# Attention then a skipping mixture of experts: one slot group closed early, 1/rms as a power on GpSimd, k^T v in small jobs

## The chip, the cores and the metric

The kernel runs on one core of a Trainium2 chip. The metric is the device time of one execution in microseconds, about 1.8 us more than the span in the profile.

The kernel before took 557.6 to 561.4 us on the chip of the first four experiments, 580.1 to 583.7 on the chip of the next four, and 579.6 to 582.2 on that of the last four. I call the first kind quiet and the others stuttering; what they differ in is shown below. The timed result of the change is, to judge by before's 558.88, from a quiet chip, while the profile of the kernel before, from which the prediction was made, is an execution of 581.39 us. So times are compared only within one call, or through their ratios to the kernel before.

## The reference

```python
kv = einsum('bhsd,bhse->bhde', k, v)            # 8 batches, 8 heads, 576 rows, 64 wide
out = einsum('bhsd,bhde->bhse', q, kv)
x = out / sqrt(mean(out*out, -1) + 1e-6) * g_norm   # then (B, H, S, D) -> (4608, 512)
do = x @ w_skip > 0                             # rows that compute
e = argmax(x @ w_gate), gate = softmax at e     # 8 experts
out[do] = x + gate * (relu(x @ w1[e]) @ w2[e])  # 512 -> 1024 -> 512, f32
```

## The kernel before

Attention goes through 36 units. A unit turns q on TensorE, multiplies it with the batch's k^T v (the gate logits ride along as nine more columns per head), squares on ScalarE, sums on VectorE and scales. Units are software pipelined: in step n the program issues the matmuls of unit n and the scaling of unit n-1. There are two PSUM buffers o_ps, so the matmuls of unit n+2 wait for the scaling of unit n.

```python
def scale(n):                                   # (cut to the core)
    nc.vector.tensor_reduce(out=rs, in_=sq, axis=AX.X, op=ALU.add)
    nc.scalar.activation(out=rs, in_=rs, func=ACT.Sqrt, scale=1.0 / D, bias=eps_t)

def norm(n):
    nc.vector.reciprocal(out=rs, in_=rs)
    nc.vector.tensor_tensor(out=xn, in0=heads(ps, 0, D), in1=r4, op=ALU.mult)
    nc.vector.tensor_tensor(out=lps[g][...], in0=heads(ps, D, KD), in1=r4, op=ALU.mult)
    nc.gpsimd.tensor_tensor(out=xb[...], in0=xn, in1=g_b, op=ALU.mult)
...
ends = [8, 18, 26, 32, 36]                      # groups of row tiles for gating
...
# at the first step of batch b: all 144 matmuls of k^T v of batch b + 1, then a VectorE copy
at(n, "pe", lambda b=b: state(b + 1))
```

After each group of row tiles, `choose`, `rank`, `number` and `settle` find the expert and the slot of every row (VectorE and small matmuls). After the last group the rows of each expert's 384 slots are gathered from memory, 108 small matmuls place the gate values, and eight experts run, each two layers of f32 matmuls.

Of the kernel before, what the change touches and what calls it, by code (L numbers as in the profile page):

```python
# [16 lines left out]
def kernel(  # L17
# [54 lines left out]
    wpool_a = ctx.enter_context(tc.tile_pool(name="wpool_a", bufs=1))  # L72
    attn = ctx.enter_context(ExitStack())
    setup = attn.enter_context(tc.tile_pool(name="setup", bufs=1))
    kv_pool = attn.enter_context(tc.tile_pool(name="kv", bufs=3))
    q_pool = attn.enter_context(tc.tile_pool(name="q", bufs=3))
    kvn_pool = attn.enter_context(tc.tile_pool(name="kvn", bufs=6))
# [3 lines left out]
    gat_pool = attn.enter_context(tc.tile_pool(name="gat", bufs=2))  # L81
    ps_o = attn.enter_context(tc.tile_pool(name="ps_o", bufs=2, space=bass.MemoryType.PSUM))
    ps_kv = attn.enter_context(tc.tile_pool(name="ps_kv", bufs=1, space=bass.MemoryType.PSUM))
    ps_q = attn.enter_context(tc.tile_pool(name="ps_q", bufs=1, space=bass.MemoryType.PSUM))
    ps_g = attn.enter_context(tc.tile_pool(name="ps_g", bufs=1, space=bass.MemoryType.PSUM))
# [52 lines left out]
    ut = setup.tile([P, P], BF16)  # L138
    nc.vector.tensor_scalar(out=ut[:, :], in0=row128_i[:, :], scalar1=part_f[:, 0:1],
                            scalar2=None, op0=ALU.is_ge)  # L140
    row128 = setup.tile([P, P], FP32)
    nc.vector.tensor_copy(out=row128[:, :], in_=row128_i[:, :])
    ones = setup.tile([P, P], BF16)
    nc.vector.memset(ones[:, :], 1.0)
    eps_t = setup.tile([P, 1], FP32)
    nc.vector.memset(eps_t[:, :], 1e-6)
    eorder = setup.tile([P, E], FP32)
# [21 lines left out]

    gw_b = setup.tile([D, 2, 4, G], FP32)  # L170
# [19 lines left out]

    w_sb = {}
# [11 lines left out]
    def state(b):  # L203

        kt, vt = kts.pop(b), vts.pop(b)
        ps = ps_kv.tile([P, 2, 512], FP32, tag="kv", name="kv_ps")
        for u in range(2):
            for c in range(C):
                for w in range(2):
                    for a in range(2):  # L210
                        r = slice(a * 64, (a + 1) * 64)
                        nc.tensor.matmul(  # L212
                            out=ps[w * 64:(w + 1) * 64, a, u * D:(u + 1) * D],
                            lhsT=kt[r, 2 * u + w, c, :], rhs=vt[r, 2 * u + w, c, :],
                            start=(c == 0), stop=(c == C - 1), skip_group_check=True)
        kvn = kvn_pool.tile([P, 2, 2, KD], FP32, tag="kvn", name="kvn")
        nc.vector.tensor_copy(out=kvn[:, :, :, 0:D],
                              in_=ps[:, :, 0:2 * D].rearrange("p a (u d) -> p a u d", u=2))
        kv_ps[b], kvns[b] = ps, kvn
# [44 lines left out]
    ends = [8, 18, 26, 32, 36]  # L264
# [37 lines left out]
    def values(n):  # L302
# [14 lines left out]
        sq = att_pool.tile([P, 2, 4, D], FP32, tag="sq", name="sq", bufs=2)  # L317
        nc.scalar.activation(out=sq[:, :, :, :], in_=heads(ps, 0, D), func=ACT.Square)  # L318
        ops[n] = (ps, sq)

    def scale(n):
        ps, sq = ops[n]
        rs = att_pool.tile([P, 2, 4], FP32, tag="rs", name="rs")
        nc.vector.tensor_reduce(out=rs[:, :, :], in_=sq[:, :, :, :], axis=AX.X, op=ALU.add)  # L324
        nc.scalar.activation(out=rs[:, :, :], in_=rs[:, :, :], func=ACT.Sqrt, scale=1.0 / D,  # L325
                             bias=eps_t[:, 0:1])
        rss[n] = rs

    def norm(n):
# [3 lines left out]
        nc.vector.reciprocal(out=rs[:, :, :], in_=rs[:, :, :])  # L333
        r4 = rs[:, :, :].unsqueeze(3)
        xn = att_pool.tile([P, 2, 4, D], FP32, tag="xn", name="xn")
        nc.vector.tensor_tensor(out=xn[:, :, :, :], in0=heads(ps, 0, D),  # L336
                                in1=r4.to_broadcast([P, 2, 4, D]), op=ALU.mult)
        g = sum(2 * nq >= x for x in ends)
        t0 = 2 * nq - ([0] + ends)[g]
        if t0 == 0 and u == 0:  # L340
            lps[g] = gat_pool.tile([P, TG, H, G], FP32, tag="lp", name="lp")
        nc.vector.tensor_tensor(out=lps[g][:, t0:t0 + 2, 4 * u:4 * u + 4, :],  # L342
                                in0=heads(ps, D, KD), in1=r4.to_broadcast([P, 2, 4, G]),
                                op=ALU.mult)
        if i is None:
            if u == 0:
                xbs[b, i] = xb_pool.tile([P, 2, DM], FP32, tag="xl", name="xl", bufs=1)
            xb = xbs[b, i]
        else:
            if i == 0 and u == 0:  # L350
                xbs[b, 0] = xb_pool.tile([P, NQ, 2, DM], FP32, tag="xb", name="xb")
            xb = xbs[b, 0][:, i, :, :]
        nc.gpsimd.tensor_tensor(  # L353
            out=xb[:, :, 4 * u * D:(4 * u + 4) * D].rearrange("p r (h d) -> p r h d", d=D),
            in0=xn[:, :, :, :],
            in1=g_b[:, :].unsqueeze(1).unsqueeze(1).to_broadcast([P, 2, 4, D]), op=ALU.mult)
        if u == 0:
            return None
# [85 lines left out]
    def columns(t0, nt, colid, val, pieces, pool):  # L444

        ohc = pool.tile([P, NT, NCOL], BF16, tag="ohc", name="ohc")[:, 0:nt, :]
# [3 lines left out]
        bv = pool.tile([P, NT, pieces, NCOL], BF16, tag=f"bv{pieces}", name="bv")[:, 0:nt, :, :]  # L450
# [6 lines left out]
    def place(ps, bv, t0, nt, pieces):  # L457

        for t in range(nt):
            for i in range(pieces):  # L460
                nc.tensor.matmul(out=ps, lhsT=oha_k[:, t0 + t, :], rhs=bv[:, t, i, :],
                                 start=(t == 0 and i == 0), stop=(t == nt - 1 and i == pieces - 1))

    def settle(g):
        t0, t1 = ([0] + ends)[g], ends[g]
        sp = ps_g.tile([P, 512], FP32, tag="g", name="slot_ps")[:, 0:NCOL]
        place(sp, bvs.pop(g), t0, t1 - t0, 2)
        sps[g] = sp

    def add_slots(g):  # L470
        nc.vector.tensor_tensor(out=srow[:, :], in0=srow[:, :], in1=sps.pop(g), op=ALU.add)

    load_kv(0)
# [4 lines left out]

    with tc.manual_schedule():
        state(0)  # L480
        state_t(0)
        turn(0)
        state_m(0)
        state_s(0)
        todo = {}

        def at(step, part, job):
            todo.setdefault((step, part), []).append(job)

        def jobs(step, part):  # L490
            for job in todo.pop((step, part), []):
                job()

        starts = {}
        for n, (_, b, i, _) in enumerate(units):
            if i is not None:
                starts.setdefault(b, n)
        for b, n in starts.items():
            if b + 1 < B:
                at(n, "pe", lambda b=b: state(b + 1))  # L500
                at(n + 1, "pe", lambda b=b: state_t(b + 1))
                at(n + 2, "pe", lambda b=b: state_m(b + 1))
                at(n + 3, "pe", lambda b=b: state_s(b + 1))
            at(n + 1, "pe", lambda b=b: turn_8(b))

            def loads(b=b):
                load_kv(b + 3)
                load_q(b + 2)
                if b + 2 == B - 1:
                    load_weights(0, wpool_a)  # L510
            at(n, "end", loads)

        n = 0
        while n <= NU or todo:
            if n + 1 < NU:
                turn(n + 1)
            if n < NU:
                values(n)
            jobs(n, "pe")
            if 1 <= n <= NU:  # L520
                store = norm(n - 1)
                if store:
                    at(n + 2, "end", store)
            if n < NU:
                scale(n)
            jobs(n, "dve")
            if n % 2 == 0 and n in ends:
                g = ends.index(n)
                choose(g)
                at(n + 1, "pe", lambda g=g: rank(g))  # L530
                at(n + 1, "dve", lambda g=g: number(g))
                at(n + 2, "pe", lambda g=g: settle(g))
                at(n + 2, "dve", lambda g=g: add_slots(g))
            jobs(n, "end")
            n += 1
# [3 lines left out]
    with tc.tile_pool(name="wpool_b", bufs=2) as wpool_b, \  # L539
         tc.tile_pool(name="gather", bufs=1) as gather_pool, \  # L540
         tc.tile_pool(name="ffn", bufs=2) as ffn, \
         tc.tile_pool(name="slot", bufs=1) as slot_pool, \
         tc.tile_pool(name="ps_i", bufs=2, space=bass.MemoryType.PSUM) as ps_i, \
         tc.tile_pool(name="ps_h", bufs=3, space=bass.MemoryType.PSUM) as ps_h, \
         tc.tile_pool(name="ps_y", bufs=3, space=bass.MemoryType.PSUM) as ps_y:

        def slot_rows():

            rows = slot_pool.tile([P, NCOL], I32, tag="rows", name="rows")
            nc.vector.tensor_single_scalar(out=rows[:, :], in_=srow[:, :], scalar=float(N),  # L550
                                           op=ALU.add)
            src = slot_pool.tile([P, NCOL], I32, tag="src", name="src")
            nc.vector.tensor_single_scalar(out=src[:, :], in_=rows[:, :], scalar=N - 1, op=ALU.min)
            return rows, src
# [15 lines left out]
        def slot_gates(colid):  # L570
            gp = ps_i.tile([P, 512], FP32, tag="xp", name="gate_ps")[:, 0:NCOL]
# [49 lines left out]
        def experts(group, colid):  # L621
# [3 lines left out]
            if group == "first":  # L625
                gates()
# [61 lines left out]
```

## Time and profile before

| | before |
|---|---|
| time, median | 558.88 us (558.57 to 559.84) |
| span of the profiled execution | 579.5 us |
| last scaling ends | 179.0 us |
| gap to layer 1 | 49 us in the profile (46.7 to its first matmul, at 225.7) |
| experts | 8 x 42.7 us |

The prediction shows the stages, waits and chain. What is still needed is the cost of one operation of each kind in a unit. The columns of the page's groups: line, engine, operation, output and input, their sizes, count | busy us, mean ns of one | idle time of the engine before them and what ended it.

```profile
L353 POOL TENSOR_TENSOR xb<-xn,g_b 128x512 f32<-128x512 f32 x32 | 40.6, 1269 | 116.0 <-DVE xn L336 115.9
L336 DVE TENSOR_TENSOR xn<-o_ps,rs 128x512 f32<-128x512 f32 x36 | 24.9, 692 | 4.2 <-DVE rs L333 0.5
L324 DVE TENSOR_REDUCE rs<-sq 128x8 f32<-128x512 f32 x36 | 24.4, 679 | 4.7 <-ACT sq L318 4.5
L325 ACT ACTIVATE rs<-rs,eps_t 128x8 f32<-128x8 f32 x36 | 10.8, 301 | 74.5 <-DVE rs L324 74.3
```

GpSimd is idle for 116 us before its one product per unit, and the square root is small but stands in ScalarE's order. Both invite the change: take work from ScalarE and VectorE and give it to GpSimd.

### The profile page before, as it was taken

The page shows a single profiled execution, that of the slowest core. Times are in us where ns is not written, and L with a number is a line of the kernel's source. Part 1 is how long each engine was busy: PE and PEld are TensorE (multiplying, and loading weights), DVE is VectorE, ACT ScalarE, POOL GpSimd, SP SyncE. Part 2 cuts the span into 40 slices and gives each one's busy share as a digit, 9 for nine tenths or more (in the row PEclk, how much of TensorE's full clock was granted, in tenths as well). Part 3 has the DMA queues.
Part 4 walks back from the last instruction along what each step waited for, and adds up shares of the span by engine and source line. Part 5 has one row for each costly group of instructions (what it writes and reads, how often), then busy time and mean ns, then how long its engine had stood idle before and what let it go on. Part 6 is the DMA issues. An engine that isn't in the chain of part 4 may idle for free.

```text
span 579.5 us, 8786 instructions
## 1 busy us (share of the span) xinstructions
PE 466.6 (81%) x3820; PEld 280.7 (48%) x3820; DVE 135.1 (23%) x351; ACT 95.2 (16%) x204; POOL 102.0 (18%) x108
## 2 busy tenths in 40 slices
PE   2576776679641316999999999999999999999990
PEld 2465655557531204545545545545545545545540
DVE  0143664742878301002002002011011011010010
ACT  0243443233342000200200100100200101101100
POOL 0022333231334770001001001001010010010010
PEclk9589877675785556999999999999999999999996
DMA  8997877583246993043044044044044000000000
GB/s 277 396 390 259 314 255 253 155 301 67 61 88 175 395 416 138 1 163 132 32 163 153 13 163 170 3 163 164 3 161 166 2 20 10 1 36 12 2 36 15
DMA packets 33131, 82.91 MB, mean 143 GB/s; under 512 B 3409, under 2 KB 3409, under 8 KB 33088
## 3 DMA queue, kind: packets, MB, share of 16 engines
q1 hardware_dynamic: 25216, 61.87, 29.7%
q0 software_dynamic: 5152, 15.66, 7.9%
q10 hardware_dynamic: 2720, 4.77, 3.5%
q8 instruction: 32, 0.52, 0.4%
q14 instruction: 11, 0.09, 0.0%
HBM read 68.21 MB, written 15.73 MB: 145 GB/s over the span
## 4 chain that ended last, share of the span: by engine, by line
PE 73%; DVE 10%; issue 6%; DMA 5%; ACT 2%; POOL 1%; POOLq 0%; DVEq 0%; ACTq 0%
PE hps L602 29%; PE yps L609 28%; PE o_ps L313 4%; PE kv_ps L212 3%; PE q_ps L278 2%; PE xp L591 2%; DMA q<-in_q_dram 2%; DVE xn L336 2%; PE kv_ps L247 2%; DMA xg<-out_dram,src 2%; DMA wraw<-in_moe_w_gate_dram 1%; DVE rs L324 1%; PE kv_ps L237 1%; DVE oha_k L439 1%; DVE lg L381 1%
## 5 line engine op out<-in xcount | busy, mean ns | idle before, releaser
L602 PE MATMUL hps<-xt,w 128*128 128x384 f32 x512 | 168.7, 488 | 0.0
L609 PE MATMUL yps<-w,ht 128*128 128x512 f32 x384 | 166.1, 592 | 0.0
L602 PEld LDWEIGHTS hps<-xt,w 128*128 128x128 f32 x512 | 96.8, 191 | 64.5 <-issue 0.8
L609 PEld LDWEIGHTS yps<-w,ht 128*128 128x128 f32 x384 | 73.0, 190 | 90.1 <-issue 88.0
L611 DVE SCALAR_TENSOR_TENSOR xg<-yps,gate,xg 128x512 f32<-128x512 f32 x24 | 18.0, 751 | 308.2 <-PE yps L609 308.2
L604 ACT ACTIVATE ht<-hps 128x384 f32<-128x384 f32 x64 | 31.4, 490 | 328.8 <-PE hps L602 284.6
L614 POOL DMA_INDIRECT out_dram<-xg,rows x24 | 23.7, 986 | 325.8 <-DVE xg L611 319.9
L353 POOL TENSOR_TENSOR xb<-xn,g_b 128x512 f32<-128x512 f32 x32 | 40.6, 1269 | 116.0 <-DVE xn L336 115.9
L313 PE MATMUL o_ps<-kvn,qT 64*64 64x73 f32 x512 | 30.7, 271 | 12.5 <-DVE lp L342 10.8
L212 PE MATMUL kv_ps<-v,k 64*64 64x64 f32 x1152 | 23.2, 245 | 18.3 <-DMA v<-in_v_dram 9.9
L313 PEld LDWEIGHTS o_ps<-kvn,qT 64*64 64x64 f32 x512 | 24.9, 168 | 20.9 <-DVE lp L342 13.3
L278 PE MATMUL q_ps<-ident,q 128*128 128x128 f32 x128 | 27.3, 350 | 9.4 <-DMA q<-in_q_dram 4.8
L212 PEld LDWEIGHTS kv_ps<-v,k 64*64 64x64 f32 x1152 | 22.3, 161 | 18.7 <-issue 18.7
L313 PE MATMUL o_ps<-kvs,qT 64*64 64x73 f32 x512 | 30.2, 271 | 0.0
L581 POOL DMA_INDIRECT xg<-out_dram,src x24 | 24.5, 1022 | 13.0 <-issue 7.0
L591 PE MATMUL xp<-ident,xg 128*128 128x128 f32 x96 | 16.5, 314 | 12.0 <-DMA xg<-out_dram,src 12.0
L278 PEld LDWEIGHTS q_ps<-ident,q 128*128 128x128 f32 x128 | 18.8, 177 | 15.1 <-ACT q L297 5.6
L336 DVE TENSOR_TENSOR xn<-o_ps,rs 128x512 f32<-128x512 f32 x36 | 24.9, 692 | 4.2 <-DVE rs L333 0.5
L324 DVE TENSOR_REDUCE rs<-sq 128x8 f32<-128x512 f32 x36 | 24.4, 679 | 4.7 <-ACT sq L318 4.5
L313 PEld LDWEIGHTS o_ps<-kvs,qT 64*64 64x64 f32 x512 | 24.4, 168 | 0.0
L325 ACT ACTIVATE rs<-rs,eps_t 128x8 f32<-128x8 f32 x36 | 10.8, 301 | 74.5 <-DVE rs L324 74.3
L318 ACT ACTIVATE sq<-o_ps 128x512 f32<-128x512 f32 x36 | 21.6, 599 | 8.3 <-PE o_ps L313 7.6
(102 smaller groups left out, 234.0 us busy)
## 6 DMA issues: line engine op xcount, KB each, us to landing
w<-in_moe_w_dram SPq DMA_DIRECT2D x16, 2048.0 KB, 8.4
k<-in_k_dram SPq DMA_DIRECT2D x8, 1152.0 KB, 11.4
v<-in_v_dram SPq DMA_DIRECT2D x8, 1152.0 KB, 12.0
q<-in_q_dram SPq DMA_DIRECT2D x8, 1152.0 KB, 9.1
out_dram<-xb POOLq DMA_DIRECT2D x8, 512.0 KB
out_dram<-xb ACTq DMA_DIRECT2D x8, 512.0 KB, 4.4
out_dram<-xl POOLq DMA_DIRECT2D x2, 256.0 KB
out_dram<-xl ACTq DMA_DIRECT2D x2, 256.0 KB, 4.0
```

What stands on the lines that cost most here:

```text
L212: nc.tensor.matmul(out=ps[w * 64:(w + 1) * 64, a, u * D:(u + 1) * D], lhsT=kt[r, 2 * u + w, c, :], rhs=vt[r, 2 * u + w, c, :], start=(c == ...
L278: nc.tensor.transpose(out=ps[:, w, hf, :], in_=qts[b][:, 2 * u + w, c:c + 2, :], identity=ident[:, :])
L313: nc.tensor.matmul(out=ps[hf * 64:(hf + 1) * 64, r, (2 * w + a) * KD:(2 * w + a + 1) * KD], lhsT=qT[rows, w, hf, a * 64:(a + 1) * 64], rhs ...
L324: nc.vector.tensor_reduce(out=rs[:, :, :], in_=sq[:, :, :, :], axis=AX.X, op=ALU.add)
L336: nc.vector.tensor_tensor(out=xn[:, :, :, :], in0=heads(ps, 0, D), in1=r4.to_broadcast([P, 2, 4, D]), op=ALU.mult)
L353: nc.gpsimd.tensor_tensor(out=xb[:, :, 4 * u * D:(4 * u + 4) * D].rearrange("p r (h d) -> p r h d", d=D), in0=xn[:, :, :, :], in1=g_b[:, : ...
L581: nc.gpsimd.indirect_dma_start(out=xg[:, c, :], out_offset=None, in_=out[:, :], in_offset=bass.IndirectOffsetOnAxis(ap=src[:, col:col + 1] ...
L591: nc.tensor.transpose(out=xp[:, dc, :], in_=xg[:, c, dc * P:(dc + 1) * P], identity=ident[:, :])
L602: nc.tensor.matmul(out=hps[:, :], lhsT=w1[:, dc, f * P:(f + 1) * P], rhs=xt[:, dc, :], start=(dc == 0), stop=(dc == DC - 1))
L604: nc.scalar.activation(out=ht[:, f, :], in_=hps[:, :], func=ACT.Relu)
L609: nc.tensor.matmul(out=yps[:, :], lhsT=ht[:, f, c * P:(c + 1) * P], rhs=w2[:, f, :], start=(f == 0), stop=(f == FC - 1))
L614: ins = nc.gpsimd.indirect_dma_start(out=out[:, :], out_offset=bass.IndirectOffsetOnAxis(ap=rows[:, col:col + 1], axis=0), in_=xg[:, c, :] ...
```

## The change

Its intent: shorten a unit, and let TensorE work in the gap. The diff is shortened to what matters here, with comments put in.

```diff
+    sqs = [setup.tile([P, 2, 4, D + 1], FP32, name=f"sq{i}") for i in range(2)]   # eps as a 65th column
     nc.vector.tensor_reduce(out=rs, in_=sq, axis=AX.X, op=ALU.add)
-    nc.scalar.activation(out=rs, in_=rs, func=ACT.Sqrt, scale=1.0 / D, bias=eps_t)
+    nc.gpsimd.tensor_tensor(out=rs, in0=rs, in1=half_t, op=ALU.pow)               # half_t = -0.5
...
-    nc.vector.reciprocal(out=rs, in_=rs)
-    nc.vector.tensor_tensor(out=xn, in0=heads(ps, 0, D), in1=r4, op=ALU.mult)
-    nc.vector.tensor_tensor(out=lps[g][...], in0=heads(ps, D, KD), in1=r4, op=ALU.mult)
+    nc.vector.tensor_tensor(out=xl, in0=heads(ps, 0, KD), in1=r4, op=ALU.mult)    # one product, 584 wide
+    # issued after the power of the next unit:
+    nc.gpsimd.tensor_tensor(out=xb[...], in0=xl[..., 0:D], in1=g_b, op=ALU.mult)
+    nc.gpsimd.tensor_copy(out=lps[g][...], in_=xl[..., D:KD])
...
-ends = [8, 18, 26, 32, 36]
+ends = [8, 18, 26, 36]
...
-at(n, "pe", lambda b=b: state(b + 1))      # 144 matmuls at once, VectorE copy
+# state(b, 0), state(b, 1), state_t, state_m, state_s in five units, ending one unit ahead; ScalarE copy
+at(max(n - 5 + i, 0), "pe", lambda b=b, part=part: part(b))
...
+# after group 2: gather expert 0's first 128 slots; after the loop:
+expert_in(xg0, xt0, 0); choose(LAST)
+layer_1(0, xt0, ht0, first, range(0, 3)); rank(LAST); number(LAST)
+layer_1(0, xt0, ht0, first, range(3, 7)); settle(LAST)
+xgs = gather_all(src, 1); layer_1(0, xt0, ht0, first, range(7, FC)); ...; yps0 = layer_2(0, ht0, 0)
...
-    place(gp, columns(...), 0, NT, 3)      # 108 matmuls of 24 columns
+    place(gp, bv, 0, NT)                   # 36 matmuls of 72 columns, pieces added by VectorE
```

The power acts on the plain sum of squares, not on the mean, so g_norm is multiplied once by the square root of 64 at the start. The slots of expert 0 that are filled by the first 26 tiles stay valid: the count of expert 0 is raised to at least 128 before the last group, so its rows go behind them.

## The prediction

> **What bounds the kernel now.** I first cut the span into its stages with a table of windows. Columns: the stretch, its length, busy microseconds of each engine with instruction counts, the granted TensorE clock, the DMA share and the rate.
>
> ```profile
> 26.20:179.00 152.80, 106.51 (x2543) 86.21 (x2542) 87.16 (x241) 59.64 (x135) 50.46 (x44) 0.77 0.66 213
> 179.00:227.90 48.90, 12.93 (x151) 10.42 (x151) 14.81 (x45) 1.73 (x2) 26.46 (x26) 0.50 0.89 326
> 227.90:566.30 338.40, 338.35 (x966) 176.49 (x965) 29.29 (x43) 31.36 (x64) 22.67 (x23) 1.00 0.21 76
> 566.30:579.50 13.20, 0.00 (x0) 0.00 (x0) 0.74 (x1) 0.00 (x0) 0.98 (x1) 0.63 0.05 16
> ```
>
> The reader sees four stages. In attention (to 179) no engine is full: TensorE 106.5 of 152.8 us, VectorE 87.2. In the gap between attention and experts TensorE works 12.9 of 48.9. In the experts it is busy without a break at full clock; only fewer matmuls would help there, and the change removes none. The tail is a last scatter. So there is time to win in the first two stages only, about 200 us.
>
> Why does attention wait? The table of waits for 28 to 174 us (who waited for whom, total, times, longest):
>
> ```profile
> ACT rs L325 <- DVE rs L324: 70.3, 26, 7.2
> DVE kvn L217 <- PE kv_ps L212: 36.2, 7, 7.0
> DVE kvn L241 <- PE kv_ps L237: 13.9, 4, 5.4
> PE o_ps L313 <- DVE lp L342: 11.6, 12, 1.8
> PE kv_ps L212 <- issue: 8.4, 3, 3.4
> ```
>
> The engines hold each other up. ScalarE stands 70 us before the square root, which needs VectorE's sum; behind it in ScalarE's order are the copy of the next turned q and the next square, so TensorE is held too. VectorE stands 36 us for k^T v, a block of 144 matmuls run as one job, and everything behind that copy waits.
>
> The gap, from the chain that ended last (start, us, what):
>
> ```profile
> 179.15 0.68 DVE lg L381
> ...
> 184.22 0.40 PE slot_ps L461 x8
> ...
> 187.29 1.05 POOL xg L581
> ...
> 189.93 8.78 DMA xg<-out_dram,src
> 198.84 1.08 PE xp L591 x4
> 199.93 1.06 PE gate_ps L461 x40
> ...
> 210.12 2.59 issue
> ...
> 222.58 1.35 PE gate_ps L461 x44
> ```
>
> Gating, then gathers, then a burst of 108 small gate matmuls that stutters: 40 of them take 1.06 us, but the middle two dozen take 21 us, in which the profile names no releaser ("issue") and the DMA share is 1.00 at 401 GB/s (window 201.0 to 222.6). The profiled span is 579.5, the timed median 559.18; with about 2 us of launch (581.39 against 579.5) the profiled execution is 22.2 us longer than a timed one. The stutter has just that size (19.1 us of "issue" before gate_ps), so I choose to put the whole difference there: a timed gap of about 26.7 us, a timed attention end still at 179.
>
> **What the Trainium skill says.** "GPSIMD Engine Reference", section Performance versus the Vector engine, gives about 2.6 cycles per element at 1.2 GHz for a two-input operation: 512 elements make 1.1 us plus dispatch. The trace agrees: the xb product of 128x512 takes 1.27 us. The page has nothing on a power. "Runtime: NRT & Kernel Launch", section Instruction fetch mechanics, says the sequencer fetches its instructions by DMA in blocks; the trace has an instruction queue of 0.52 MB, and its TensorE stutters just where the DMA share is 1.00. That fetch is starved there is my inference. "TensorE: Matmul & The Clock Gate", Part 1, says that idling halves the clock; the trace grants 0.50 in the gap, 0.77 in attention and 1.00 in the experts.
>
> **The change, part by part.**
>
> (1) 1/rms. Removed: 36 square roots on ScalarE (301 ns each, 10.8 us) with their 70 us of standing, 36 reciprocals (0.19) and 36 products lp (0.22) on VectorE, 14.8 us. Added: 36 powers of 128x8 on GpSimd and 36 copies of 128x72; the scaling takes 584 columns where it took 512, 0.69 x 584/512 = 0.79 us; the sum takes 520 for 512, 0.69. No row shows a power on GpSimd. Its small operations take 0.1 to 0.2 us (iota 128x8: 0.13); for the power I assume 0.5 us, for the copy 0.25, both estimates. A unit's cycle on VectorE becomes sum 0.69, power with two hand-overs 0.7, scaling 0.79: 2.2 us. GpSimd per unit: 0.5 + 1.27 + 0.25 + a quarter of a store's issue (0.65 + 0.3), 2.3 us. They are level.
>
> (2) k^T v. The same 1152 matmuls, in jobs of 72, five units ahead, and the copy kvn (8 x 0.42) goes to ScalarE. The five steps of a batch's state now stand in five units, before anything wants them, so the 36 and 13.9 us of standing should mostly go.
>
> Attention then: 36 x 2.2 = 79 us of cycles; three groups' gating inside the loop, 7.0 us for ten tiles (3.0 choosing from 105.62, 4.0 numbering from 110.19), about 6.2 for each of two groups of eight, 19.4, less 4 where it covers the power's latency; 8 x 0.4 of small copies: 98 us. The first sum can start at about 29, so VectorE alone gives an end at 127. TensorE's 106.5 us from 26 gives 133. Loads, stores and the first weights, 41.9 MB at the 390 GB/s of the early slices, end at 9 + 107 = 116. Three limits so close, each engine in order, cost more than the largest; I choose 14 us for that: attention ends at **147** instead of 179.
>
> (3) The gap. The last group now has ten tiles, so its chain is longer: product and copy 1.6, choosing 3.0, ranking 0.7, numbering 4.0, placing and adding 1.1, rows 0.4, sum 11 us; then gathers, whose second reached TensorE 7.7 us after the first was issued (187.29 to 194.95); transposes and copies 1.8, and the gates, 36 matmuls of 72 columns where there were 108 of 24, about 1.5. Sum **22** us until layer 1 starts on the other 256 slots. Inside it TensorE does the first 128 slots of expert 0: a third of 20.5 and of 20.6 us (layers 1 and 2 from the chain), **13.7** us. An extra gather in the loop makes GpSimd wait once for stores to land (a store from ScalarE 4.4 us), counted in the 14.
>
> (4) The rest. From the first layer-1 matmul to the last matmul 340.5 us before (225.72 to 566.26), less 13.7: 327. The tail keeps 13.2, plus 0.5 for the count of rounds, now after the last result.
>
> Sum: 147 + 22 + 327 + 13.7 + 2 = **about 511**; I say 510. Against 559: 32 from attention, 5 from a shorter gap, 13.7 from work moved into it.
>
> **Rivals.**
> - **The power is slow.** Each microsecond over 0.5 lies on the cycle sum, power, scaling and adds about 36 us. At 1.5 us attention ends at 183, and only the gap pays: 546. For it: no view shows the operation, and software evaluates it. Against: just 8 elements a lane.
> - **Transfers become the limit.** A batch of 13 us needs 4.7 MB, 363 GB/s of the 390 seen. Then attention ends late (155 to 160), TensorE stutters on "issue" more often, as it did before kv_ps, and the time is 520 to 525.
> - **The stutter is real in timed runs too.** Then the old gap was near 45 us and attention ended earlier than 179 when timed; with a third of the gate matmuls, and the weights loaded while gating runs, the new gap loses nearly all of it: 490 to 495.
> - **Attention only swaps its waits**, TensorE at a low clock becoming the bound: end at 165, time 528.
>
> **Range and chances.** Power 0.3 to 1.0 us, and an end of attention between 130 and 168, give 490 to 532; I say 488 to 534. Even with nothing gained in attention, the moved work gives about 14 of the 11 us that 2% are, so faster has 0.95, same 0.03, slower 0.02.
>
> **What would show it.** Right: no wait of ScalarE on the sum; k^T v without a long wait of the copy; the last scaling near 147 us; layer 1 of 128 columns running during choosing and numbering; layer 1 of 256 columns some 22 us after the last scaling; the profiled span close to the timed one, as the stutter goes. Wrong: a power over 1 us with VectorE waiting for it; TensorE waiting for xb or o_ps at an unchanged pace; DMA at 1.00 throughout attention; gathers that land late behind the weights.

## The result, and the profile after

The changed kernel takes **550.78 us** (547.66 to 551.39, four runs) against 558.88. The ratio is 0.984, with a 95% interval of 0.9806 to 0.9874: the mean time of one kernel's fast runs over that of the other's of the same rounds, so not quite the ratio of the medians. That is 1.6% faster, within the 2% that count as the same, and outside the range of 488 to 534. The gain is 8 us where 49 were forecast. Executions in which one die ran at a lower clock are left out of the means.

The same table of windows as in the prediction, for the changed kernel, cut at its own stage ends:

```profile
28.00:181.80 153.80, 105.81 (x2493) 86.15 (x2492) 73.56 (x150) 53.38 (x104) 115.35 (x115) 0.76 0.76 265
181.80:203.40 21.60, 19.61 (x154) 15.01 (x154) 15.59 (x40) 2.55 (x9) 10.77 (x12) 0.89 0.42 115
203.40:533.10 329.70, 327.21 (x964) 175.83 (x964) 31.01 (x44) 30.59 (x64) 37.84 (x40) 1.00 0.26 92
533.10:545.90 12.80, 0.00 (x0) 0.00 (x0) 1.54 (x6) 0.00 (x0) 0.98 (x1) 0.70 0.05 17
```

The gap did what was asked of it: 21.6 us long, TensorE busy for 19.6 of them. Attention did not: it ends at 181.8, later than before (179.0). VectorE works less in it (73.6 us) and GpSimd more than twice as much (115.4, where the kernel before had 50.5).

The table of waits for 28 to 174 us, the window of the prediction, shows what replaced the old ones:

```profile
POOL rs L335 <- DVE rs L334: 52.7, 19, 26.5
DVE xl L344 <- POOL rs L335: 44.6, 24, 3.0
ACT qT L290 <- PE q_ps L287: 43.5, 27, 5.1
...
PE o_ps L322 <- DVE xl L344: 13.7, 10, 2.7
...
DVE kvn L250 <- PE kv_ps L246: 10.4, 4, 3.0
...
DVE lg L391 <- POOL lp L366: 9.4, 3, 3.2
```

ScalarE's 70 us before the square root are gone and so are VectorE's 36 before k^T v, as intended. In their place VectorE stands 45 us for the power; over the whole of attention it is 48.9 us, in 26 of 36 units. The last line is new as well: at each of the three groups VectorE waits about 3 us for GpSimd's copy of the logits (lp), which now stands behind a power and an xb in GpSimd's order. The chain that ended last shows one unit after the other (start, us, what):

```profile
134.73 0.61 DVE rs L334
135.34 0.07 issue
135.41 1.65 POOL rs L335
...
137.08 0.04 DVE xl L344
137.12 0.65 issue
137.77 0.69 DVE rs L334
...
138.53 1.64 POOL rs L335
```

Sum, power, scaling, next sum: from one power to the next 3.12 us. The scaling shows as the 0.04 of xl and the 0.65 of "issue", since the next sum starts 0.69 us after it and waited for nothing but its own engine. More than half of this cycle is the power. Not every unit runs at it: of the 35 intervals between sums 17 are 3.1 to 3.2 us long, and the mean is 4.23, as other intervals hold gating or other waits. The page has the power in one row:

```profile
L335 POOL TENSOR_TENSOR rs<-rs,half_t 128x8 f32<-128x8 f32 x36 | 59.3, 1646 | 61.1 <-DVE rs L334 52.9
```

1.65 us for eight columns, where the prediction had assumed 0.5.

### The profile page after: what moved, and what is told of

It is laid out like the page before. It is cut to its first block, busy times and chain, and to the rows that moved or that the text cites. A ratio compares the mean times of both kernels' runs of the same rounds, so it can differ in the third digit from the quotient of the medians.

```text
span 545.9 us, 8655 instructions
## 1 busy us (share of the span) xinstructions
PE 462.9 (85%) x3776; PEld 285.4 (52%) x3776; DVE 124.7 (23%) x265; ACT 89.8 (16%) x182; POOL 168.1 (31%) x183
## 4 chain that ended last, share of the span: by engine, by line
PE 69%; DVE 12%; POOL 9%; issue 4%; DMA 4%; ACT 1%; POOLq 0%; DVEq 0%
PE hps L634 30%; PE yps L641 29%; POOL rs L335 6%; DVE rs L334 3%; DMA q<-in_q_dram 2%; PE o_ps L322 2%; DVE xl L344 2%; PE kv_ps L219 2%; DMA wraw<-in_moe_w_gate_dram 2%; PE q_ps L287 2%; PE xp L619 1%; POOL xb L362 1%; DVE xt L621 1%; DVE oha_k L449 1%; DVE ohc L457 1%
## 5 line engine op out<-in xcount | busy, mean ns | idle before, releaser
L634 PE MATMUL hps<-xt,w 128*128 128x384 f32 (+2 forms) x576 | 169.6, 456 | 4.3 <-DVE xt L621 4.3
L634 PEld LDWEIGHTS hps<-xt,w 128*128 128x128 f32 x576 | 106.5, 195 | 67.4 <-DVE xt L621 4.9
L636 ACT ACTIVATE ht<-hps 128x384 f32<-128x384 f32 (+2 forms) x72 | 32.8, 456 | 303.0 <-PE hps L634 294.8
L335 POOL TENSOR_TENSOR rs<-rs,half_t 128x8 f32<-128x8 f32 x36 | 59.3, 1646 | 61.1 <-DVE rs L334 52.9
L621 DVE COPY xt<-xp 128x512 f32<-128x512 f32 x24 | 15.8, 687 | 137.0 <-PE xp L619 136.7
L322 PE MATMUL o_ps<-kvn,qT 64*64 64x73 f32 x512 | 31.4, 271 | 14.7 <-DVE xl L344 9.9
L362 POOL TENSOR_TENSOR xb<-xl,g_b 128x512 f32<-128x512 f32 x32 | 39.8, 1243 | 0.0
L344 DVE TENSOR_TENSOR xl<-o_ps,rs 128x584 f32<-128x584 f32 x36 | 27.6, 766 | 49.1 <-POOL rs L335 48.9
L322 PEld LDWEIGHTS o_ps<-kvn,qT 64*64 64x64 f32 x512 | 25.3, 168 | 22.7 <-issue 12.5
L334 DVE TENSOR_REDUCE rs<-sq 128x8 f32<-128x520 f32 x36 | 24.7, 686 | 12.3 <-ACT sq L327 12.3
L327 ACT ACTIVATE sq<-o_ps 128x512 f32<-128x512 f32 x36 | 21.5, 598 | 35.8 <-PE o_ps L322 34.8
L290 ACT COPY qT<-q_ps 128x512 f32<-128x512 f32 x32 | 18.8, 586 | 52.5 <-PE q_ps L287 48.1
```

What stands on the lines that cost most here:

```text
L322: nc.tensor.matmul(out=ps[hf * 64:(hf + 1) * 64, r, (2 * w + a) * KD:(2 * w + a + 1) * KD], lhsT=qT[rows, w, hf, a * 64:(a + 1) * 64], rhs ...
L334: nc.vector.tensor_reduce(out=rs[:, :, :], in_=sq[:, :, :, :], axis=AX.X, op=ALU.add)
L335: nc.gpsimd.tensor_tensor(out=rs[:, :, :], in0=rs[:, :, :], in1=half_t[:, :, :], op=ALU.pow)
L344: nc.vector.tensor_tensor(out=xl[:, :, :, :], in0=heads(ps, 0, KD), in1=r4.to_broadcast([P, 2, 4, KD]), op=ALU.mult)
L362: nc.gpsimd.tensor_tensor(out=xb[:, :, 4 * u * D:(4 * u + 4) * D].rearrange("p r (h d) -> p r h d", d=D), in0=xl[:, :, :, 0:D], in1=g_b[:, ...
L634: nc.tensor.matmul(out=hps[:, cols], lhsT=w_sb[e][0][:, dc, f * P:(f + 1) * P], rhs=xt[:, dc, cols], start=(dc == 0), stop=(dc == DC - 1))
```

## The experiments

The main theory: the power's latency in the chain sum, power, scaling took all that the smoother schedule gave. Rivals: something else (TensorE at its low clock, transfers) held a unit at 3 us; GpSimd was simply full; or the gap's work was given back. All outputs are right.

**e1, the power by itself.** Ahead of attention, while the loads are under way (the three tiles and their fills are left out):

```diff
+    for i, m in enumerate((1, 4, 8, 16, 32)):
+        nc.gpsimd.tensor_tensor(out=pout[:, i, 0:m], in0=pin[:, 0:m], in1=pex[:, 0:m], op=ALU.pow)
+    nc.gpsimd.tensor_tensor(out=pout[:, 4, 32:40], in0=pin[:, 0:8], in1=pex[:, 0:8], op=ALU.mult)
```

> The changed kernel with five extra powers on GpSimd ahead of attention, of 1, 4, 8, 16 and 32 columns (128 lanes each), and one product of 8 columns, all before the loads land. If the 1.64 us of a 128x8 power is a fixed cost of the operation, all five take 1.5 to 1.9 us. If it is paid per element (about 0.2 us a column), they take about 0.3, 0.9, 1.6, 3.2 and 6.4 us. The product of 8 columns should take 0.15 to 0.25 us either way. The end of the kernel should not move by more than 3 us.

One run, 553.11 us. The groups of GpSimd by form, 2 to 14 us:

```profile
L527 POOL TENSOR_TENSOR pout<-pin,pex 128x32 f32<-128x32 f32 x1 | 5.4, 5418 | 0.0
L527 POOL TENSOR_TENSOR pout<-pin,pex 128x16 f32<-128x16 f32 x1 | 2.9, 2890 | 0.0
L527 POOL TENSOR_TENSOR pout<-pin,pex 128x8 f32<-128x8 f32 x1 | 1.6, 1627 | 0.0
L527 POOL TENSOR_TENSOR pout<-pin,pex 128x4 f32<-128x4 f32 x1 | 1.0, 1021 | 0.0
L527 POOL TENSOR_TENSOR pout<-pin,pex 128x1 f32<-128x1 f32 x1 | 0.6, 578 | 0.1
...
L528 POOL TENSOR_TENSOR pout<-pin,pex 128x8 f32<-128x8 f32 x1 | 0.2, 196 | 0.0
```

Between the two theories: from 1 to 32 columns 4.84 us are added, 0.156 us a column, on a base of about 0.42. A product of eight columns takes 0.20, so the power costs eight times as much as the operation that it resembles.

**e2 and e14, the square root back.** All else of the change stays.

```diff
-        nc.gpsimd.tensor_tensor(out=rs[:, :, :], in0=rs[:, :, :], in1=half_t[:, :, :], op=ALU.pow)
+        nc.scalar.activation(out=rs[:, :, :], in_=rs[:, :, :], func=ACT.Sqrt)
...
+        nc.vector.reciprocal(out=rs[:, :, :], in_=rs[:, :, :])
```

> The changed kernel with the square root back on ScalarE and the reciprocal back on VectorE (everything else of the change stays). Theory A, the power of 1.64 us sits in the cycle sum, power, scaling and alone sets the 3.1 us of a unit: without it the cycle is 0.68 + 0.3 + 0.2 + 0.77 + hand-overs, about 2.3 us, and attention ends near 150 instead of 181.8, the time is 515 to 522. Theory B, the power took the place of the old waits by chance and something else (TensorE at its low clock, the transfers) holds a unit near 3 us anyway: attention ends at 172 or later, time 541 or more.

527.93 us against 559.95, ratio 0.946 (0.939 to 0.953). Attention and gap in the table of windows:

```profile
28.00:161.00 133.00, 100.55 (x2488) 82.02 (x2480) 79.64 (x186) 58.41 (x141) 55.04 (x81) 0.82 0.88 306
161.00:183.00 22.00, 18.98 (x154) 14.37 (x154) 15.19 (x39) 3.73 (x10) 11.07 (x11) 0.92 0.49 132
```

Attention ends at 160.9, 20.9 us sooner than with the power; the gap is the same. This is theory A, though less strongly than it said: the end was expected near 150 and the time at 515 to 522. The waits of e2:

```profile
ACT rs L335 <- DVE rs L334: 31.2, 20, 3.9
DVE rs L334 <- ACT sq L327: 28.7, 18, 4.1
DVE rs L342 <- ACT rs L335: 12.8, 24, 3.9
```

ScalarE stands before the square root again, but 31 us and not 70, and no wait carries the rest alone. To have changed kernel and square root on one chip, both ran again:

> The changed kernel, unaltered, as the anchor for the other three of this call, since the chips of the first two calls differ by 20 us in the kernel before (559 and 583 us). Attention should end at 181 to 183 us on any chip. Theory: the chip decides whether TensorE stutters on issue while weights and gathers fill the DMA engines. On a chip where before takes about 559, this takes 549 to 553; on one where before takes about 582, 555 to 562.

> The kernel of e2 once more, beside the changed kernel on one chip. Attention ends at 160 to 162; the time lies 19 to 24 us under that of the unaltered changed kernel of this call, which is what the power costs. If the difference of e2 came from the chip instead, under 8 us.

Here, on a stuttering chip, before took 580.94 us, the changed kernel 561.08 (ratio 0.966, 0.963 to 0.970) and the square root 541.02 (0.933, 0.929 to 0.937). Attention ended at 182.2 and 163.4. So the power costs 20.1 us in time, and the expectation of 19 to 24 held; the end of attention came a little later than the 160 to 162 expected. Without the power, 12 of the 35 intervals between sums in e2 are 1.9 to 2.3 us long, and their mean is 3.69 where the changed kernel had 4.23.

**e7, the power alone.** The kernel before with nothing but the other 1/rms (eps as a column, power on GpSimd, no root and reciprocal).

> The kernel before with only 1/rms changed: sum with eps as a column, power on GpSimd, no square root, no reciprocal. Theory A: a power of 1.64 us against a square root and a reciprocal of 0.5 us lengthens each dependent cycle by about 1.2 us, some of which lies beside the old waits for k^T v: 10 to 30 us slower than before, 569 to 589. Theory B: the power is free where other waits ruled: within 4 us of 559.

596.17 us against 582.59, ratio 1.025 (1.020 to 1.030): 13.6 us slower, within the 10 to 30 of theory A; attention ends at 194.1 instead of 179.0. In this order of issue the power also queues behind xb on GpSimd: its chain repeats scaling 0.70, xb 1.27, power 1.61. The part of the change that issues xb after the next unit's power should therefore be needed with it; no run tests that part alone.

**e5 and e6, the small jobs undone**, together with their early start and the copy on ScalarE, once with the power and once with the square root (shortened):

```diff
-                at(max(n - 5 + i, 0), "pe", lambda b=b, part=part: part(b))
+                at(starts[b - 1] + i, "pe", ...)      # i = 0, 0, 1, 2, 3
-        nc.scalar.copy(out=kvn[...
+        nc.vector.tensor_copy(out=kvn[...
```

> The changed kernel (power on GpSimd kept) with k^T v back as one job of 144 matmuls in the first step of the batch before, its four steps as early as before, and the copy kvn back on VectorE. Theory A, a unit is held near 3.1 us by the power: the small jobs have slack to fill and undoing them costs under 5 us (551 to 556), attention ends at 182 to 187. Theory B, the small jobs carry a gain of their own beside the power: attention ends at 192 or later, time over 560.

> The same undoing on the kernel of e2 (square root on ScalarE), whose attention ends at 161. Theory A: where the power no longer holds a unit, the small jobs are worth more: 8 to 15 us slower than e2 (536 to 543), with the long wait of VectorE for k^T v back in the table of waits. Theory B: they are worth nothing here either, within 3 us of 528, and the gain of e2 over before comes from the other edits of the units (one product for two, the copy of logits on GpSimd).

e5: 568.75 us, ratio 0.980 (0.974 to 0.986); attention ends at 188.4. e6: 553.12 us, ratio 0.951 (0.946 to 0.956); attention ends at 172.7. Both belong to a stuttering chip, so they are compared with e13 and e14, from another chip of that kind: attention ends 6.2 us later with the power and 9.3 us later without it, and by the ratios undoing costs 1.4% and 1.9%. VectorE's wait for k^T v is back in both. The line of e6:

```profile
DVE kvn L226 <- PE kv_ps L219: 33.2, 7, 6.5
```

So the small jobs have a gain of their own. By the ends of attention the power hides about a third of it; the intervals of the ratios are too wide to show that in time. Theory A for e6; for e5 the end fell between the two bands.

**e10, GpSimd relieved.** The product xb moves to VectorE, into the time in which VectorE waits.

```diff
-        nc.gpsimd.tensor_tensor(
+        nc.vector.tensor_tensor(
             out=xb[:, :, 4 * u * D:(4 * u + 4) * D]...
```

> The changed kernel with the product xb of 128x512 on VectorE, in the time in which it waits for the power. GpSimd keeps power and copy, 1.9 us a unit instead of 3.1. If the latency of the chain sum, power, scaling holds a unit, it stays at 3.1 us and attention ends at 179 to 186. If GpSimd being full holds it, a unit falls toward 2.5 us and attention ends at 170 or earlier.

564.59 us, ratio 0.971 (0.968 to 0.974), 3.5 us slower than the changed kernel of its call; attention ends at 184.1. GpSimd was not the limit by being full: without xb its work in a unit is a power of 1.95 and a copy of 0.32 us, it stands idle for 93 us before the powers instead of 61, and attention goes no faster. What it shows besides, in the rows of the tile rs:

```profile
L335 POOL TENSOR_TENSOR rs<-rs,half_t x36: 1683/1948/2021, 30.2 to 181.4; 128x8 f32<-128x8 f32 x36
```

The power itself went from a median of 1.64 to 1.95 us while VectorE ran products with two inputs in SBUF, and the cycle with it from 3.12 to 3.49. The Trainium skill, "GPSIMD Engine Reference", section Key points, names that contention; this is its size here.

**e8, another order on VectorE.** The kernel of e2 with the sum of unit n issued before the scaling of unit n-1.

> The kernel of e2 with VectorE's order in a step swapped: the sum of unit n ahead of the scaling of unit n-1, so that square root and reciprocal latency lie beside the other unit's work. If the latency of the cycle still sets the pace, 5 to 12 us faster than e2 (516 to 523). If the two buffers of o_ps do (the scaling that frees one now waits behind the next sum), no gain or slower, 528 to 540.

571.43 us, ratio 0.982 (0.978 to 0.986). That is a large loss beside the 0.933 of the same kernel without the swap, also on a stuttering chip (e14), and more than the 0 to 12 us that the second theory allowed. Attention ends at 194.5, and its chain repeats o_ps 1.29, square 0.61, sum 0.69, scaling 0.78, with hand-overs 3.85 us a unit (starts of the scaling 181.18, 185.03, 188.88). The scaling that frees a buffer for TensorE now waits for the sum of the unit which TensorE has just computed. Hiding the latency by swapping was closed by the two buffers, as the second theory said of the cause.

**e3, no early work.** The changed kernel without the early gather and the first 128 slots in the gap; expert 0 does all 384 slots after it.

```diff
-        expert_in(xg0, xt0, 0)
-        layer_1(0, xt0, ht0, first, range(0, 3))        # and the two that follow
-        xgs = gather_all(src, 1)
+        xgs = gather_all(src, 0)
-        yps0 = layer_2(0, ht0, 0)
```

> The changed kernel without the early work of expert 0: no early gather, all 384 slots after gating. Expert 0's first 128 slots cost 13.7 us of TensorE; if all of that is hidden in the gap now, this one is 12 to 15 us slower than the changed kernel (563 to 566). If the early part is mostly given back (by the wait for the early gather in attention, the smaller matmuls, the longer last group), under 6 us slower.

562.52 us against 559.95, ratio 1.005 (1.001 to 1.010). Its ratio over that of the changed kernel is 1.022, so the early work is worth about 12 us; the two profiled spans differ by 14.7 (560.6 and 545.9), but the profiled execution of the changed kernel is its fastest, 3.1 us under the median. The 13.7 us were moved into the gap nearly whole. Without them the change would have been no gain at all.

**e4, merged gate matmuls on the kernel before.** 36 of 72 columns for 108 of 24, the same for the slots.

> The kernel before with only the gate and slot matmuls merged: 36 matmuls of 72 columns for 108 of 24. If the stutter of 20 us in the profile of before is in the profiled execution alone, the timed runs gain 2 to 4 us (555 to 557). If it is there in timed runs too, they gain 12 to 18 us (541 to 547), and attention in timed runs of before ended earlier than 179 us. In the profile the gap from the last scaling to layer 1 should fall from 49 to about 27 us under the first theory.

557.81 us, ratio 0.999 (0.993 to 1.005): the same. This was on a quiet chip, and its trace has no stutter: the last scaling ends at 178.0, layer 1 starts at 201.8, a gap of 24 us where the profile before had 46.7. The trace of e7, with the 108 small matmuls and on a stuttering chip, has the stutter again (19.0 us of "issue" before gate_ps, 19.1 in the profile before). The chip of the profile before is not on record, and the unaltered kernel before was not profiled on a quiet chip; but its time and these two traces say that its stutter belongs to a stuttering chip and not to profiling, and that the gap in the timed runs was near the 26.7 that the prediction chose. On stuttering chips the pause did not go with the small matmuls. In e13 the chain has it inside layer 1 of expert 0:

```profile
205.93 9.90 PE hps L634 x32
216.24 8.79 another core or an unknown queue
225.49 5.72 PE hps L634 x16
```

Layer 1 of these 256 slots takes 25.3 us there (205.93 to 231.21) and 14.1 in the quiet trace, so it loses about 11 us where the kernel before lost 19 to 22. That difference is about the 12 us by which the change gains more on such a chip (3.4%, 19.9 us) than on a quiet one (1.6%, 8.1 us).

**e12, a better version tried.** The kernel of e2 with ranking one step later and settling two.

> The kernel of e2 with the ranking of a group one step later and its settling two, so that TensorE does not stand before the slot matmuls for VectorE (6.6 us in e2) and the early gather comes later too. If TensorE's order is what holds attention there, it ends at 152 to 157 and the time is 4 to 8 us under the kernel of e2 of this call. If VectorE's own gating work is the limit, within 3 us of it.

540.00 us, ratio 0.928 (0.924 to 0.931). Against e14's 541.02 it can't be told apart. Attention did end 3 us sooner (160.4), but the pauses in layer 1, 7.2 and 1.6 us against 5.1, took most of it back.

**The best that was run is the change with the square root kept: 527.93 us on a quiet chip, 541.02 on a stuttering one, faster than both kernels; e12 equals it within the noise.**

## Why the prediction was wrong

**Power, the step that failed.** "for the power I assume 0.5 us" was an estimate from the small operations of GpSimd in the trace, none of which is a power. It takes 1.64 us. The cycle, given as 2.2 us, is 3.12. That cost 20.9 us of attention (e2) and 20.1 us of time on one chip (e13 and e14), all that the smoother schedule gave and a little more. The wait for the copy of the logits (9.4 us, and 0.9 in e2) is probably part of it; the prediction has no term for it. The other estimate, 0.25 us for that copy itself, held. (The prediction's 1.1 us for a product of 512 columns is an estimate too, from the page that it names; its sums use the measured 1.27.)

**The end of attention, 147, the other failed term.** Even without the power it comes at 160.9. The 14 us chosen for three engines in order should have been 28. The sum of 36 x 2.2 us takes every unit to run at the cycle; a cycle near 2.2 is there in e2, but in 12 of 35 intervals only. Lowering one wait of 70 us left 31 of it, and others of 29 and 13 us came up; TensorE, at a granted clock of 0.82, was busy for 100.6 of 133 us. I know of no single cause for this, and it stays open; in the two profiles, e12's order of TensorE at the groups is worth about 3 us of it. The rival "Attention only swaps its waits" gave 165 and 528, near e2's 160.9 and 527.93; that the low clock is the bound, as it said, no run shows.

**The rival "the power is slow"** named the mechanism, and at 1.5 us gave 546. At 1.64 its own rule gives 147 + 1.14 x 36 = 188 and 551. The close agreement is partly luck: the power costs 20.9 us and not 41, since most units without it take longer than 2.2 us (3.69 on average in e2), and the 14 us beside it were too few. The weight given to it was too small, with the range cut at a power of 1.0.

**k^T v**: right in kind; the wait of 36 us is gone. Worth 9.3 us at the end of attention, and 6.2 beside the power.

**The gap**: 22 predicted, 21.6 measured (181.8 to 203.4). Its first term held: the chain from last scaling to rows took 11.2 us (181.8 to 193.0), predicted 11. The second half has the right size by another path. The prediction has layer 1 wait for gathers (7.7 us), transposes and gates; in the trace no transpose waits for a gather, and the chain goes through VectorE's work on the gate values, beside which TensorE does layer 2 of the early slots:

```profile
193.48 0.34 ACT ex L597
...
197.20 2.93 DVE bv L461
...
200.18 1.36 PE gate_ps L470 x36
...
202.69 0.69 DVE xt L621
...
203.42 0.70 PE hps L634 x2
```

So that agreement is luck in part, and in this trace a faster gather would not have shortened the gap. The timed stage ends of before were chosen well: the longer profile came, as far as e4 and e7 show, from the chip that it ran on.

**Moved work**: 13.7 predicted, about 12 measured by the ratios and 14.7 by the two profiled spans (e3). **The rest**: 327 predicted, 329.7 measured. Each later expert takes 43.12 us (starts of layer 1 at 276.23 and 319.35) where it took 42.70: the transposes now stand between the layers, and TensorE waits there for a copy of xt. Seven times 0.42 make the 3 us.

**The sum.** For the profiled execution: attention +34.8, the gap -0.4, experts +2.7, tail -0.9, makes 36 over the sum of 511: 547, and it took 547.66. Its four timed runs' median is 3.1 us higher, with spans of 548.1 to 549.6 in the others at a granted clock of 0.89 to 0.91 instead of 0.92. I have not looked for the cause of this.

**Faster at 0.95** was wrong as well. "Even with nothing gained in attention, the moved work gives about 14" left out that attention could get worse and the experts longer: +2.8 and +3 us against 13.7 and a gap 2 to 5 us shorter. That leaves 10 to 13; 8 to 11 were measured.

## What to carry to other kernels

An operation which no row of the profile shows deserves a run of its own before it is put into a dependent cycle; its cost counts once per cycle, however idle its engine is. An idle engine is a place for work off the chain (xb), not for a step between two dependent operations of a busier engine; even the copy of the logits made VectorE wait 3 us at each group, because it stood behind a power. When several parts of a change meet in one cycle, undo them one at a time: here one part took back the gain of the others, and the sum looked as if little had happened. And check the path as well as the number: the gap came out at the predicted length by another chain.

## What the Trainium skill lacked or had wrong

- "GPSIMD Engine Reference" has no cost for a power. Measured: 0.58, 1.02, 1.63, 2.89 and 5.42 us for 1, 4, 8, 16 and 32 columns of 128 lanes, against 0.20 for a product of eight.
- The same page, Key points, names the contention of GpSimd with VectorE operations of two SBUF inputs, without a size for it here: the power went from 1.64 to 1.95 us, the copy of 72 columns from 0.25 to 0.32 (e10).
- "Runtime: NRT & Kernel Launch", Instruction fetch mechanics, calls the cost of crossing from one fetched block to the next mostly hidden. In the trace of before TensorE pauses for 19.1 us in all with no releaser, at a DMA share of 1.00; in e7 it is 19.0 us at 0.95. But the 5.1 us pause of e14 (200.2 to 205.3) stands at a share of 0.73. That it is fetching is still an inference; no run here separates it.
- No page that I read says that chips differ in this: with one kernel, 557.6 to 561.4 us on one chip and 579.6 to 583.7 on two others. Why is open.
